# Sums of denominators and the decay of token sums on GpSimd, a half chunk of maxima turned with 128 rows, column sums inverted once

## The chip, the cores and the metric

The kernel runs on one core of a Trainium2 chip. The metric is the time of one execution on the device, in microseconds. A core has engines that each run their own instructions in order and wait for one another by semaphores: PE (TensorE), DVE (VectorE), ACT (ScalarE), POOL (GpSimd) and SP (SyncE, here only DMA issues).

## The reference

An attention whose softmax has one extra term in its denominator, followed by a soft mixture of experts with 32 slots (8 experts with 4 slots each). Sizes: 8 batches, 12 heads, 448 tokens, 64 dimensions a head; 3584 tokens of width 768 for the second part; hidden width 1024.

```python
m = max(scores, axis=-1); e = exp(scores - m)
attn = e / (sum(e) + exp(-m) + 1e-09)          # x = attn @ v, heads side by side
logits = x @ phi                               # 3584 x 32
d = exp(logits - logits.max(0)); d /= d.sum(0) + 1e-09     # over the tokens, for each slot
c = exp(logits - logits.max(1)); c /= c.sum(1) + 1e-09     # over the slots, for each token
slot_out[e] = relu((d.T @ x)[e] @ w1[e]) @ w2[e]
out = c @ slot_out
```

## The kernel before

**The attention** is worked off in 48 pairs of heads, six pairs to a batch, three pairs to a group that is loaded together. The 448 tokens of a head lie in chunks of 128, 128, 128 and 64 rows; the fourth, half chunks of both heads of a pair share one tile of 128 rows. For a pair n there are these stages, each a small function:

- `T(n)` turns q and k on PE into a tile of psA (PSUM, three banks, shared with everything tagged "a"); ACT or DVE copies it out (L255, L257).
- `A(n, i)` or `A1(n, i, hl)`: scores in one orientation on PE (L274, L283, L291), and DVE takes the row maxima straight from psA into the tile `wm` (L277, L285, L292). These run about six pairs ahead.
- `W2(g)` and `W3(g)`, once in three steps: PE turns the group's maxima `wm` (three full chunks at L299, the half chunk at L302), ACT copies them to `mT`, and computes exp(-m) into `ec` (L311, L314).
- `AB(n, i)` and `Bk`: scores in the other orientation less the maxima (L359 and L362, L337 and L340) and ACT's exponential (L364, L343). `AB` sets two score matmuls of `A1` around them.
- `AV(n, i, qs)`: e times v on PE into one bank (psV). A column of ones in v gives the sums of e as column D of each of the seven blocks.
- `N1(n)`: ACT copies that bank to `ubuf` (L409; DVE for the last pairs, and none for the very last).
- `N2(n)`: DVE adds 1e-9, the sum and `ec` (L418, one instruction on 128x7) and inverts (L419); POOL multiplies u by the result into x (L423, L427, L428). `on_pool(n)` is true for n < 44; for the last four pairs DVE multiplies.
- `PX(n)`: PE turns x (L449), ACT copies it (L455).
- `V(g)`: POOL copies v of a group into place (L378 to L381).

**The second part**, `P(b)`, goes on beside the attention, one batch behind it, in six steps spread over half steps of the loop: logits (`l_mm`, `l_ev`, `c_max`), their running maximum (`l_turn`, `s_max`), the differences (`c_sub` L507 and `d_sub` L519 on POOL), `exps` and `corr` on ACT, then `both(s_mm, fade, s_add)`: PE computes the batch's token sums (`ps_s`, in psA), `fade` multiplies the accumulator `acc` (128x224) by the decay exp(old maximum - new maximum) (L534, DVE), and `s_add` adds (L557, DVE). `c_turn` turns the second softmax's exponentials, sums them for each token (L551, DVE), adds 1e-9 and inverts (L552, L553) into `crec`, which is read only near the end of the program (L840). The name `eng` in `P` is POOL for the first six batches and DVE for the last two. After the last pair come the experts (`hidden`, `turn`, `slots`) and the output.

**The order of the work is written out by hand.** Every engine's instructions run in the order in which the loop emits them: for s in 0 to 47 and y in 0 and 1, the scores of pair s, AV of pair s-1 or s, at y = 0 `N1(s-1)`, at y = 1 `T(s+6)`, once in three steps (s = 2, 5, 8, ...) `W2` and `W3`, the step of `P` that is due (`post`), and then `N2(s-1)`, since it is on POOL. At the end of a step POOL gets its loads and copies: at s = 2, 5, 8, ... q and k of a group (two DMA issues, L162); at s = 3, 6, 9, ... `V` of a group, v of the next (two issues, L166 and L167) and, for most of them, a half of a weight (L111); at s = 1, 4, 7, ... another half of a weight. These DMA issues are POOL instructions of 0.7 to 0.8 us each. `s_mm`, `fade` and `s_add` of batch b come at y = 1 of s = 6b + 10.

In `wm` the half chunks of the two heads lie in one column, head 1 in rows 0 to 63 and head 0 in rows 64 to 127.

Of the kernel before, what the change touches and what calls it, by code (L numbers as in the profile page):

```python
# [8 lines left out]
F32 = mybir.dt.float32  # L9
BF16 = mybir.dt.bfloat16  # L10
AX = mybir.AxisListType
AF = mybir.ActivationFunctionType
ALU = mybir.AluOpType
# [12 lines left out]
NP = 3  # L26
# [5 lines left out]
def kernel(  # L32
# [10 lines left out]
    nc = tc.nc  # L43
    B, H, S, D = q.shape
    DD = H * D
    NS = moe_phi.shape[1]
# [3 lines left out]
    KC = DD // 128  # L50
# [15 lines left out]
    crec = keep.tile([128, B, 4], F32, name="crec")  # L66
    acc = keep.tile([128, KC + 1, NS], F32, name="acc")

    ident = const.tile([128, 128], BF16, name="ident")
# [5 lines left out]
    halfm = const.tile([128, 2], F32, name="halfm")  # L75
# [67 lines left out]
    with ExitStack() as at:  # L143
        pool = lambda name, bufs, **kw: at.enter_context(tc.tile_pool(name=name, bufs=bufs, **kw))
        psm = pool("small", 2)
# [77 lines left out]
        nc.gpsimd.memset(ones, 1.0)  # L223
        nc.gpsimd.memset(ones[64:128, 1:2], 0.0)

        ec, mT, eT, av, us = {}, {}, {}, {}, {}
        qkT = {}
        st = {"e2": 0}

# [32 lines left out]
        mg = lambda n: 0 if n == 0 else n // NP + 1  # L262
# [32 lines left out]
        def W2(g):  # L295
            w = wm[g % 2]
            ps = pb_("ps_m")
            for i in range(3):
                nc.tensor.matmul(ps[:, i * 128:(i + 1) * 128], w[:, i, :], ident, start=True, stop=True)  # L299
            for hl in range(2):  # L300
                r = slice(64 - 64 * hl, 128 - 64 * hl)
                nc.tensor.matmul(ps[64 * hl:64 * hl + 64, 384:448], w[r, 3, 0:64], ident[r, r], start=True, stop=True)  # L302
            st["ps_m"] = ps

        def W3(g):
            t = psm.tile([128, S], BF16, tag="mT", name="mT")
            nc.scalar.copy(t, st["ps_m"][:, 0:S])
            mT[g] = t
            e = psm.tile([128, NP, 7], F32, tag="ec", name="ec", bufs=3)
            w = wm[g % 2]  # L310
            nc.scalar.activation(e[:, :, 0:6].rearrange("p l (i h) -> p i l h", i=3),  # L311
                                 w[:, 0:3, :].rearrange("p i (h c) -> p i c h", h=2)[:, :, 0:NP, :],
                                 AF.Exp, scale=-scale)
            nc.scalar.activation(e[:, :, 6], w[:, 3, 0:NP], AF.Exp, scale=-scale)  # L314
            ec[g] = e


# [83 lines left out]
        on_pool = lambda n: n < NPAIR - 4  # L401

        def N1(n):
            src = av[n][:, 0:7 * W65].rearrange("p (s c) -> p s c", c=W65)
            if n == NPAIR - 1:
                us[n] = src
                return
            u = ubuf[:, n % 2, :].rearrange("p (s c) -> p s c", c=W65)
            (nc.scalar.copy if on_pool(n) else nc.vector.tensor_copy)(u, src)  # L409
            us[n] = u  # L410

        def N2(n):
            g, pl = divmod(n, NP)
            b, pb = divmod(n, PB)
            u = us[n]
            eng = nc.gpsimd if on_pool(n) else nc.vector
            rec = psm.tile([128, 7], F32, tag="rec", name="rec", bufs=3)
            nc.vector.scalar_tensor_tensor(rec, u[:, :, D], 1e-9, ec[mg(n)][:, pl, :], op0=ALU.add, op1=ALU.add)  # L418
            nc.vector.reciprocal(rec, rec)  # L419
            x = xb[b % 2]  # L420
            c = pb * 128
            rec2 = psm.tile([128, 2], F32, tag="rec2", name="rec2", bufs=3)
            eng.tensor_mul(  # L423
                x[:, 0:3, c:c + 128].rearrange("p i (h d) -> p i h d", h=2),
                u[:, 0:6, 0:D].rearrange("p (i h) d -> p i h d", h=2),
                rec[:, 0:6].rearrange("p (i h) -> p i h", h=2).unsqueeze(3).to_broadcast([128, 3, 2, D]))
            eng.tensor_scalar(rec2, halfm, rec[:, 6:7], None, op0=ALU.mult)  # L427
            eng.tensor_mul(  # L428
                x[:, 3, c:c + 128].rearrange("p (h d) -> p h d", h=2),
                u[:, 6, 0:D].unsqueeze(1).to_broadcast([128, 2, D]),  # L430
                rec2.unsqueeze(2).to_broadcast([128, 2, D]))
# [30 lines left out]
        def P(b):  # L462
            l, new = lb[b % 2], lb[(b + 1) % 2][:, 4, :]
            eng = nc.gpsimd if b < B - 2 else nc.vector
            x = xb[b % 2]
            v = {}
# [64 lines left out]

            def fade():
                if b:
                    nc.vector.tensor_mul(acc, acc, v["corr"].unsqueeze(1).to_broadcast([128, KC + 1, NS]))  # L534

            def s_mm(j0=0, j1=KC + 1):
                ps = pa([128, j1 - j0, NS], F32, "ps_s")
# [8 lines left out]
            def c_turn():  # L546
                ps = pa([128, 128], BF16, "ps_ct")
                nc.tensor.transpose(ps, flat(v["cd"][:, 0:4, :]), ident)
                nc.vector.tensor_copy(cT[:, b // 2, :, b % 2, :], ps.rearrange("p (h j) -> p h j", h=2))
                r = crec[:, b, :]  # L550
                nc.vector.reduce_sum(r, v["cd"][:, 0:4, :], axis=AX.X)  # L551
                nc.vector.tensor_scalar(r, r, 1e-9, None, op0=ALU.add)  # L552
                nc.vector.reciprocal(r, r)  # L553

            def s_add():
                if b:
# [89 lines left out]
        for s in range(NPAIR):  # L646
            for y in range(2):
                hs = 2 * s + y
                early, last_ = int(hs < 5), int(hs < 3)
                if early:  # L650
                    As(1)
                    Bk(s, 2 * y)
                    warm(int(hs < 2), S)
                    As(1)
                    Bk(s, 2 * y + 1)
                    warm(int(hs < 2), S)
                    As(1)
                elif s < NPAIR:
                    AB(s, 2 * y)
                    if y:  # L660
                        Bk(s, 3, 1)
                    else:
                        AB(s, 1)
                if hs < 5:
                    T(hs + 3)
                if y == 0:
                    if 0 <= s - 1:
                        for i in (2, 3):
                            AV(s - 1, i, range(3))
                else:  # L670
                    if 2 <= s < NPAIR - 6:
                        T(s + 6)
                    g = (s + 1) // 3
                    if (s + 1) % 3 == 0 and g < NG:
                        W2(g + 1)
                        W3(g + 1)
                    if s < NPAIR:
                        for i in (0, 1):
                            AV(s, i, range(3))
                if 2 * s + y in post:  # L680
                    post[2 * s + y]()
                if hs == 2 * (NPAIR - 2) + 1:
                    nc.vector.reduce_max(fold, ident.rearrange("p (i s) -> p s i", i=4), axis=AX.X)
                if y and 0 <= s - 2 < NPAIR - 2 and s - 2 != n6:
                    PX(s - 2)
                if hs == 2 * n6 + 4:
                    PX(n6)
                if y == 0:
                    if 0 <= s - 1:
                        for i in range(4):  # L690
                            AV(s - 1, i, [3])
                        N1(s - 1)
                        if not on_pool(s - 1):
                            N2(s - 1)
                else:
                    if 0 <= s - 1 and on_pool(s - 1):
                        N2(s - 1)
                As(last_)
                if hs == 1:
                    W2(1)  # L700
                    W3(1)
            g = (s + 10) // 3
            if s == 1 or s % 3 == 2:
                g = 3 if s == 1 else g
                if (s == 1 or g > 3) and g < NG:
                    load(g, "q")
                    load(g, "k")
            g = (s + 9) // 3
            if s % 3 == 0 and g - 2 < NG:
                V(g - 2)  # L710
                if s and g - 1 < NG:
                    load(g - 1, "v")
            if s == 1:
                load(2, "v")
            if s == 0:
                for z in range(2, 4):
                    narrow(z)
            if s in half_at:
                load_half(half_at[s], 0, w_tile(half_at[s]))
            if s - 2 in half_at:  # L720
                load_half(half_at[s - 2], 1)
            if s in narrow_at:
                narrow(narrow_at[s])
            for i, z0, z1 in part_at.get(s, ()):
                load_part(i, z0, z1)
            for i, z0, z1 in col_at.get(s, ()):
                load_first(i, z0, z1)
        n = NPAIR - 1
# [3 lines left out]
        AV(n, 3, range(4))  # L732
        load_second(0, 4)
        N1(n)
        N2(n)
        PX(n - 1)
        last[0]()
# [47 lines left out]
        h = [h0, h1]  # L785
# [50 lines left out]
        for half in range(2):  # L836
            ps = psA.tile([128, 512], F32, tag="a", name="ps_cs")
            r = slice(64 * half, 64 * half + 64)
# [57 lines left out]
```

## Time and profile before

| | |
|---|---|
| runs | 308.66, 308.94, 310.42 us (median 308.94) |
| profiled execution | 309.52 us, its span 307.7 us |
| mean granted TensorE clock | 0.955 |
| busy of the span | PE 91%, DVE 84%, ACT 82%, POOL 60% |
| L418 and L419 on DVE | 48 x 0.154 and 48 x 0.201 us |
| L423, L427, L428 on POOL | 44 x 0.823, 0.286 and 0.398 us |
| L534 on DVE | 7 x 0.382 us |
| L552 and L553 on DVE | 8 x 0.170 and 8 x 0.178 us |
| L302 on PE | 34 x 0.213 us |

The span runs from the first to the last instruction; the rest of the execution's time lies around it. A line of the order of time gives start, time from the start of the first to the end of the last of a run of like instructions, engine, line, operation, output and input with their shapes, and in square brackets how long the engine sat idle before it and what ended that. The chain that ended last is followed back from the last instruction, at each step to what released it. The 30 to 225 us in which the loop has its full set of work is called the steady part here.

### The profile page before, as it was taken

The numbers are of one execution on the slowest core, as the hardware profiler recorded it, in microseconds if no ns is written. First come the engines' busy times: TensorE is split into PE (matmuls) and PEld (weight loads), VectorE is DVE, ScalarE is ACT, GpSimd is POOL, SyncE is SP. The second block draws the span as 40 slices with busy tenths as digits, with TensorE's granted clock in tenths as the row PEclk, the third lists the DMA queues.
The fourth block names the chain that finished last, engine by engine and source line by source line (L and its number), as shares of the span: only waits on it lengthen the run. The fifth ranks groups of instructions, "written<-read, shape, count | busy, mean of one in ns | idle before, by whom it ended". The sixth has DMA issues, their size and how long they took to land.

```text
span 307.7 us, 12173 instructions
## 1 busy us (share of the span) xinstructions
PE 279.3 (91%) x5097; PEld 159.8 (52%) x5097; DVE 257.1 (84%) x604; ACT 250.9 (82%) x551; POOL 184.9 (60%) x336
## 2 busy tenths in 40 slices
PE   7999999999999999999999999999999999995900
PEld 2444656566565656555656565656564555441100
DVE  7899999999999999989999999999999676446910
ACT  3477999999999999989999999999999995345800
POOL 9681986968586869866877677686747662000000
PEclk9999999999999999999999999999999999997555
DMA  8999999999999999999999999999845899909995
GB/s 134 134 158 184 139 210 202 195 197 165 191 161 198 164 200 148 202 184 151 120 202 134 197 179 204 151 200 205 141 56 88 124 137 224 362 32 341 433 426 229
DMA packets 49384, 57.69 MB, mean 188 GB/s; under 512 B 2865, under 2 KB 41521, under 8 KB 48945
## 3 DMA queue, kind: packets, MB, share of 16 engines
q0 software_dynamic: 45280, 42.29, 89.6%
q1 hardware_dynamic: 4048, 14.62, 12.1%
q8 instruction: 40, 0.66, 0.8%
q14 instruction: 16, 0.12, 0.1%
HBM read 88.18 MB, written 14.16 MB: 333 GB/s over the span
## 4 chain that ended last, share of the span: by engine, by line
PE 69%; DVE 14%; ACT 8%; issue 3%; POOL 1%; DVEq 0%; POOLq 0%
PE ps_av L397 15%; PE ps_a L291 9%; PE ps_t L251 7%; PE ps_b L359 7%; PE ps_b L362 6%; DVE R L292 6%; PE ps_b L337 4%; PE ps_b L340 2%; ACT R L343 2%; DVE R L277 2%; PE ps_x L449 2%; PE ps_o L802 2%; PE ps_a L274 2%; PE ps_so L773 2%; ACT R L255 2%
## 5 line engine op out<-in xcount | busy, mean ns | idle before, releaser
L292 DVE TENSOR_REDUCE R<-ps_a 128x1 bf16<-128x448 f32 x254 | 140.0, 615 | 6.4 <-PE ps_a L291 5.5
L364 ACT ACTIVATE R<-ps_b 128x448 bf16<-128x448 f32 x272 | 131.0, 573 | 0.5 <-PE ps_b L362 0.2
L291 PE MATMUL ps_a<-R 64*128 64x448 bf16 x254 | 83.2, 353 | 1.5 <-DVE R L292 1.5
L359 PE MATMUL ps_b<-R 64*128 64x448 bf16 x272 | 74.5, 353 | 1.1
L362 PE MATMUL ps_b<-mT,sel 64*128 64x448 bf16 x272 | 71.3, 350 | 0.0
L423 POOL TENSOR_TENSOR R<-ubuf,rec 128x384 bf16<-128x384 f32 x44 | 36.2, 823 | 55.1 <-DVE rec L419 33.7
L397 PEld LDWEIGHTS <-R 128*128 128x128 bf16 (+1 forms) x1536 | 50.0, 100 | 30.8 <-issue 26.1
L397 PE MATMUL ps_av<-R 128*128 128x65 bf16 (+1 forms) x1536 | 64.6, 196 | 0.0
L343 ACT ACTIVATE R<-ps_b 128x448 bf16<-128x448 f32 x64 | 35.9, 579 | 2.7 <-PE ps_b L340 2.6
L251 PEld LDWEIGHTS <-R 64*64 64x64 bf16 x1344 | 30.0, 112 | 12.6 <-issue 4.9
L455 ACT CAST R<-ps_x 128x512 bf16<-128x512 f32 x47 | 28.1, 599 | 6.9 <-PE ps_x L449 6.4
L251 PE MATMUL ps_t<-ident,R 64*64 64x64 bf16 x1344 | 31.2, 196 | 0.6
L285 DVE TENSOR_REDUCE R<-ps_a 128x1 bf16<-128x448 f32 x48 | 29.6, 617 | 0.6 <-PE ps_a L283 0.6
L362 PEld LDWEIGHTS <-sel 64*128 64x128 bf16 x272 | 21.8, 94 | 15.1 <-issue 5.5
L291 PEld LDWEIGHTS <-R 64*128 64x128 bf16 x254 | 23.8, 94 | 11.1 <-issue 1.1
L409 ACT COPY ubuf<-ps_av 128x455 f32<-128x455 f32 x44 | 25.1, 570 | 2.4 <-POOL R L428 2.2
L255 ACT COPY R<-ps_t 128x896 bf16<-128x896 bf16 x20 | 18.4, 922 | 6.0 <-PE ps_t L251 5.6
L337 PE MATMUL ps_b<-R 64*64 64x448 bf16 (+1 forms) x112 | 21.9, 375 | 0.0
L277 DVE TENSOR_REDUCE R<-ps_a 128x1 bf16<-128x448 f32 x34 | 18.9, 618 | 2.1 <-PE ps_a L274 2.0
L340 PE MATMUL ps_b<-mT,sel 64*64 64x448 bf16 (+1 forms) x112 | 20.5, 353 | 0.0
L428 POOL TENSOR_TENSOR R<-ubuf,rec 128x128 bf16<-128x128 f32 x44 | 17.5, 398 | 3.7
L359 PEld LDWEIGHTS <-R 64*128 64x128 bf16 x272 | 17.2, 94 | 4.7 <-issue 0.3
(137 smaller groups left out, 439.7 us busy)
## 6 DMA issues: line engine op xcount, KB each, us to landing
W<-in_moe_w_dram POOLq DMA_DIRECT2D x22, 768.0 KB, 10.2
R<-in_v_dram POOLq DMA_DIRECT2D x32, 192.0 KB, 4.9
out_dram<-W SPq DMA_DIRECT2D x2, 2688.0 KB, 11.8
R<-in_q_dram POOLq DMA_DIRECT2D x14, 336.0 KB, 7.9
R<-in_k_dram POOLq DMA_DIRECT2D x14, 336.0 KB, 9.0
wd<-in_moe_w_dram POOLq DMA_DIRECT2D x8, 384.0 KB, 10.7
R<-wd SPq DMA_DIRECT2D x8, 384.0 KB, 8.2
R<-in_moe_w_dram POOLq DMA_DIRECT2D x2, 768.0 KB, 8.1
```

The costliest lines, as they stand in the source:

```text
L251: nc.tensor.transpose(ps[r, a, c:c + 64], src[r, pl, tok * D:(tok + 1) * D], ident[r, r])
L285: nc.vector.reduce_max(top(n, i), ps[:, 0:S], axis=AX.X)
L291: nc.tensor.matmul(ps[:, 0:S], t[r, 0, i * 128:(i + 1) * 128], t[r, 1, :], start=True, stop=True)
L292: nc.vector.reduce_max(top(n, i, hl), ps[:, 0:S], axis=AX.X)
L337: nc.tensor.matmul(outs[hl], t[rs[hl], 1, cols], t[rs[hl], 0, :], start=True, stop=False)
L343: nc.scalar.activation(e, p[:, 0:S], AF.Exp, scale=scale)
L359: nc.tensor.matmul(ps[hl][:, 0:S], t[rs[hl], 1, cols], t[rs[hl], 0, :], start=True, stop=False)
L362: nc.tensor.matmul(ps[hl][:, 0:S], sel[rs[hl], pl:pl + 1].to_broadcast([64, 128]), mT[mg(n)][rs[hl], :], start=False, stop=True)
L364: nc.scalar.activation(e[:, hl, :], ps[hl][:, 0:S], AF.Exp, scale=scale)
L397: nc.tensor.matmul(o, eT[n, i, hl][:, qc], vp[g % 2][:, 2 * pl + hl, i, 0:W65], start=(i == 0 and u == 0 and hl == 0), stop=(i == 3), skip ...
L423: eng.tensor_mul(x[:, 0:3, c:c + 128].rearrange("p i (h d) -> p i h d", h=2), u[:, 0:6, 0:D].rearrange("p (i h) d -> p i h d", h=2), rec[: ...
L455: nc.scalar.copy(xT[:, pb, :], pss[0])
```

## The change

- In `W2`, the half chunk is turned by two matmuls over all 128 rows of `wm`, each picking its 64 rows by 64 columns of the identity, instead of two over 64 rows.
- `W3` ends with POOL adding 1e-9 to `ec`.
- A new `N2a(n)` adds the sums to `ec`, on POOL for n < 44 and on DVE for the last four. It is emitted right after `N1`, half a step ahead of `N2`. `N2` begins with DVE's inversion and is otherwise as before.
- `fade` runs on `eng`, so on POOL for batches 1 to 5 and on DVE for batches 6 and 7 (batch 0 has none).
- `c_turn` only sums; the last one adds 1e-9 and inverts for all eight batches at once (128x32).

```diff
@@ W2
             for hl in range(2):
-                r = slice(64 - 64 * hl, 128 - 64 * hl)
-                nc.tensor.matmul(ps[64 * hl:64 * hl + 64, 384:448], w[r, 3, 0:64], ident[r, r], start=True, stop=True)
+                c = 64 - 64 * hl
+                nc.tensor.matmul(ps[64 * hl:64 * hl + 64, 384:448], w[:, 3, 0:64], ident[:, c:c + 64], start=True, stop=True)
@@ W3
             nc.scalar.activation(e[:, :, 6], w[:, 3, 0:NP], AF.Exp, scale=-scale)
+            nc.gpsimd.tensor_scalar(e, e, 1e-9, None, op0=ALU.add)
             ec[g] = e
@@ N2
+        def N2a(n):
+            rec[n] = psm.tile([128, 7], F32, tag="rec", name="rec", bufs=3)
+            (nc.gpsimd if on_pool(n) else nc.vector).tensor_add(rec[n], us[n][:, :, D], ec[mg(n)][:, n % NP, :])
+
         def N2(n):
...
-            rec = psm.tile([128, 7], F32, tag="rec", name="rec", bufs=3)
-            nc.vector.scalar_tensor_tensor(rec, u[:, :, D], 1e-9, ec[mg(n)][:, pl, :], op0=ALU.add, op1=ALU.add)
-            nc.vector.reciprocal(rec, rec)
+            r = rec[n]
+            nc.vector.reciprocal(r, r)
@@ fade
-                    nc.vector.tensor_mul(acc, acc, v["corr"].unsqueeze(1).to_broadcast([128, KC + 1, NS]))
+                    eng.tensor_mul(acc, acc, v["corr"].unsqueeze(1).to_broadcast([128, KC + 1, NS]))
@@ c_turn
-                r = crec[:, b, :]
-                nc.vector.reduce_sum(r, v["cd"][:, 0:4, :], axis=AX.X)
-                nc.vector.tensor_scalar(r, r, 1e-9, None, op0=ALU.add)
-                nc.vector.reciprocal(r, r)
+                nc.vector.reduce_sum(crec[:, b, :], v["cd"][:, 0:4, :], axis=AX.X)
+                if b == B - 1:
+                    nc.vector.tensor_scalar(crec, crec, 1e-9, None, op0=ALU.add)
+                    nc.vector.reciprocal(crec, crec)
@@ the loop, y == 0 (and the same line after the last pair)
                         N1(s - 1)
+                        N2a(s - 1)
                         if not on_pool(s - 1):
                             N2(s - 1)
```

## Prediction before the run

> **What bounds the kernel now.** I read first the busy times and the chain that ended last, then the busy times in stretches of 15 us, then POOL, DVE and PE in order of time through one step. The page:
>
> ```profile
> PE 279.3 (91%) x5097; PEld 159.8 (52%) x5097; DVE 257.1 (84%) x604; ACT 250.9 (82%) x551; POOL 184.9 (60%) x336
> PE 69%; DVE 14%; ACT 8%; issue 3%; POOL 1%; DVEq 0%; POOLq 0%
> L423 POOL TENSOR_TENSOR R<-ubuf,rec 128x384 bf16<-128x384 f32 x44 | 36.2, 823 | 55.1 <-DVE rec L419 33.7 <-ACT R L364 9.1 <-ACT R L255 7.1
> ```
>
> PE carries the chain, with 14% handed to DVE. POOL looks as if it had room: 60% busy, and 55.1 us of waiting before its multiplications, mostly for DVE's reciprocal. The stretches show how tight the others are (PE, PEld, DVE, ACT, POOL busy, then granted clock, DMA share, GB/s):
>
> ```profile
> 150.00:165.00 15.00, 14.88 (x319) 9.71 (x319) 14.06 (x34) 14.04 (x33) 10.63 (x21) 1.00 1.10 177
> ```
>
> From 30 to 225 us, PE, DVE and ACT are each busy 13 to 15 us of every 15. Six pairs take 30.25 us (reciprocal of pair 24 at 149.19, of pair 30 at 179.44), so a step is 5.04 us on average. The average hides what decides here, namely that POOL's work comes in bursts. In POOL's order of time, from the multiplications of pair 23 to those of pair 24:
>
> ```profile
> 144.44 0.82 POOL L423 TENSOR_TENSOR R<-ubuf,rec 128x384 bf16<-128x384 f32 x1 [0.79 <-DVE rec L419]
> 145.25 0.28 POOL L427 TENSOR_SCALAR rec<-halfm,rec 128x2 f32<-128x2 f32 x1
> 145.62 0.40 POOL L428 TENSOR_TENSOR R<-ubuf,rec 128x128 bf16<-128x128 f32 x1
> 145.96 0.66 POOL L378 COPY R<-R 128x576 bf16<-128x576 bf16 x1
> 146.68 0.66 POOL L379 COPY R<-R 128x576 bf16<-128x576 bf16 x1
> 147.29 0.34 POOL L380 COPY R<-R 64x192 bf16<-64x192 bf16 x1
> 147.69 0.34 POOL L381 COPY R<-R 64x192 bf16<-64x192 bf16 x1
> 147.98 0.73 POOL L166 DMA_DIRECT2D R<-in_v_dram  x1
> 148.70 0.67 POOL L167 DMA_DIRECT2D R<-in_v_dram  x1
> 149.35 0.78 POOL L111 DMA_DIRECT2D W<-in_moe_w_dram  x1
> 150.20 0.82 POOL L423 TENSOR_TENSOR R<-ubuf,rec 128x384 bf16<-128x384 f32 x1
> ```
>
> The last line waited for nothing but its own queue: pair 24's reciprocal was done at 149.39, and POOL was still issuing a weight load until 150.13. In each third step, at the end of steps s = 3, 6, 9 and so on, POOL runs V and the loads for 4.2 us and is late. Today that is free, since what is late is only the scaling of x, which PE reads over 2 us later (pair 24: scaled by 151.78, read from 153.96). DVE and PE at the same time:
>
> ```profile
> 149.00 0.16 DVE L418 SCALAR_TENSOR_TENSOR rec<-ubuf,ec 128x7 f32<-128x7 f32 x1
> 149.19 0.20 DVE L419 RECIPROCAL rec<-rec 128x7 f32<-128x7 f32 x1
> 149.31 2.17 DVE L292 TENSOR_REDUCE R<-ps_a 128x1 bf16<-128x448 f32 x4
> ```
> ```profile
> 149.57 0.54 PE L362 MATMUL ps_b<-mT,sel 64*128 64x448 bf16 x2
> 149.94 0.35 PE L291 MATMUL ps_a<-R 64*128 64x448 bf16 x1
> ```
>
> PE's fourth score matmul after the reciprocal starts at 149.94, 0.18 after its place in the 0.19 us rhythm (149.57 + 0.19 = 149.76) and right after the first reduction (about 149.31 to 149.85): it needs that bank of psA. So behind the reciprocal there is no slack; whatever delays it delays PE.
>
> **The sum of the denominators (N2a), the main part.** It takes 44 L418 instructions of 0.155 us from DVE and puts 44 adds on POOL, issued right after the ACT copy, and one add of 128x21 for each group. DVE's reciprocal then waits for POOL, and behind it in DVE's order stand the next six reductions of L292, which free psA for PE. In POOL's order the add stands behind all that the last step put there, so in the third steps behind the burst. An add of 128x7 on POOL is not in the trace. The nearest rows are 0.286 us (128x2 TENSOR_SCALAR) and 0.398 (128x128 TENSOR_TENSOR); the two TENSOR_TENSOR sizes (0.398 and 0.823 for 384) extrapolate to 0.19 for none. I take 0.30, with ends 0.19 and 0.40. To it come 0.07 from POOL's last instruction (150.13 to 150.20) and about 0.10 to reach DVE (the other way it is 0.15: 144.28 to 144.44). So the new reciprocal starts 0.47 after POOL is free:
>
> | pair | POOL free | reciprocal now | then | late |
> |---|---|---|---|---|
> | 3 | 44.87 | 43.99 | 45.34 | 1.35 |
> | 6 | 58.90 | 58.03 | 59.37 | 1.34 |
> | 9 | 73.82 | 73.45 | 74.29 | 0.84 |
> | 12 | 88.89 | 88.02 | 89.36 | 1.34 |
> | 18 | 120.00 | 118.26 | 120.47 | 2.21 |
> | 24 | 150.13 | 149.19 | 150.60 | 1.41 |
> | 30 | 180.39 | 179.44 | 180.86 | 1.42 |
> | 36 | 210.63 | 209.68 | 211.10 | 1.42 |
>
> Together 11.3 us. The delay does not depend on where the step begins: POOL's burst itself starts from the previous reciprocal (0.20 + 0.15 + 1.52 of multiplications + 4.2 + 0.47 = 6.5 us from reciprocal to reciprocal, against 5.1 now). In the two other steps of three POOL is free in time, or nearly; pairs 1, 11, 20 and 35 come 0.7 to 0.9 late, of which 0.34 is free (at 144.28, after pair 23's reciprocal, DVE itself waits 0.34 for PE). I count 1.6 for these.
>
> **The decay (fade) on POOL.** Five of the seven L534 (0.38 us) leave DVE, those of batches 1 to 5. Each stands in POOL's order directly behind N2a of pairs 15, 21, 27, 33, 39, again third steps, and DVE's s_add (L557) waits for it, ahead of the reciprocal.
>
> ```profile
> 163.96 0.38 DVE L534 TENSOR_TENSOR acc<-acc,corr 128x224 f32<-128x224 f32 x1
> 164.44 0.39 DVE L557 TENSOR_TENSOR acc<-acc,ps_s 128x224 f32<-128x224 f32 x1
> 164.75 0.16 DVE L418 SCALAR_TENSOR_TENSOR rec<-ubuf,ec 128x7 f32<-128x7 f32 x1
> ```
>
> On POOL, 128x224 lies between the rows of 0.398 and 0.823. From L428 to L423 the time grows by 1.66 ns an element (0.56 for 224), from L507 (128 elements, 0.415) to L519 (160, 0.539) by 3.9 (0.79); I take 0.65. The reciprocal then starts 0.07 + 0.30 + 0.65 + 0.10 + 0.31 (s_add, 164.44 to 164.75) = 1.43 after POOL is free: pair 15, 104.04, late 1.71; pair 21, 133.56, late 0.30 (no weight load there); pair 27, 166.29, late 2.78; pair 33, 195.45, late 1.70; pair 39, 224.94, late 0.95. Together 7.4 us. The Trainium skill (GPSIMD Engine Reference, section Engine selection) calls two-input elementwise work about 2x slower on GpSimd than on VectorE. The rows here say 1.36 to 1.47 (398 to 293, 823 to 558 ns). By the page's factor the fade would be an estimated 0.76, and five of them 0.5 us more in all.
>
> **What is won.** The chain passes through DVE right where the column sums are inverted:
>
> ```profile
> 139.63 0.17 DVE L552 TENSOR_SCALAR crec<-crec 128x4 f32<-128x4 f32 x1
> 139.83 0.18 DVE L553 RECIPROCAL crec<-crec 128x4 f32<-128x4 f32 x1
> ```
>
> These 0.35 and the L418 behind them (0.15) go in six steps (pairs 10, 16, ... 40); PE waited only 0.24 for DVE there before its own work is next late, so I take 0.35 each, 2.1 us. L418 alone in the six steps of pairs 7, 13, ... 37, where the chain also runs through DVE: 0.15 each, 0.9. Elsewhere L418 was off the chain (ACT and PE). The one inversion at the end (128x32, about 0.4 for both instructions) stands under the hidden layer's matmuls: nothing; without that cover 0.1.
>
> **The half chunk (L302).** Two matmuls of 64 rows become two of 128 rows; the chain gives them 0.15 us beside 0.27 for the three before. Ends: 0 and 0.15 for 15 groups in the steady part; I take 0.10, 1.5 us. The Trainium skill (TensorEngine Tiling (Array Packing), Key Properties) says that changing the tiling mode drains the array. Its rule would put the gain near the upper end, 2.3 us; that moves the sum by 0.8.
>
> **Sum.** Lost 11.3 + 1.6 + 7.4 = 20.3; I take nine tenths of it for PE (some steps have a little slack, and a gap of 1.02 us in POOL's burst of pair 27 may close): 18.3. Won 2.1 + 0.9 + 1.5 = 4.5. Net +13.8 on the profiled execution's 309.5 (span 307.7): 323.3. The median of the runs is 308.9, 0.6 lower; I give **323**. With POOL's unknowns at their ends (13 adds by -0.11 or +0.10, five fades by -0.25 or +0.17) and between seven and ten tenths reaching PE, 316 to 328.
>
> **Rivals.**
> - *Half absorbed.* The steps after a late one catch up, because DVE has about 0.5 us less to do in them and PE finds three full banks emptied back to back. For it: DVE's work falls by 11 us in all. Against: after pair 24 the chain is PE's own work (150.11 to 154.12), which starts late. Half of 20.3 less 4.5 gives +5.7: 315 (311 to 317).
> - *Faster.* POOL's add is in time, or its lateness is covered by psA: three banks hold 3 x 0.54 = 1.6 us of reductions. This decides where PE has over 1.4 us of other work ready, before it needs a fourth bank. Then only the 4.5 won is left: 304.5 (302 to 307). For it: two steps in three, where POOL waited for DVE. Against: 149.94 above, where PE already waits for that bank.
> - *No difference.* About a quarter of the delay reaches PE, equal to what is won: 309.
>
> **Chances.** Forecast 0.66, half absorbed 0.15, no difference 0.07, faster 0.12. A measurement tells 0.5% (1.5 us) from no change. Faster 0.12, same 0.07, slower 0.81. The range takes in the forecast's spread and most of the half-absorbed case: 310 to 330, leaving out the faster case, part of no difference, and a longer tail if several steps lose more than POOL's lateness.
>
> **What would show it.** The reciprocal of pairs 3, 6, 9 ... starts right after a POOL add, with DVE idle 1 to 3 us before it, released by POOL: some 15 to 20 us in the table of waits. In the five fade steps DVE waits at s_add instead. POOL's 33.7 us of waiting for the reciprocal shrinks in those steps. Cycles from reciprocal to reciprocal: 6.5 in the third steps, 7.5 or more with a fade. DVE's busy time falls by about 11 us. The forecast is wrong if the add lands before the burst, if an add takes far from 0.3, or if DVE waits and PE's span does not grow with it.

## The result, and the profile after

The changed kernel takes 325.8 us (median; 322.9 to 329.2) against 309.0 before: a ratio of 1.050, 95% interval 1.042 to 1.059. Ratios here and below are of mean times, and executions over 1.5% above the fastest of their kernel (here 329.2 us) are left out of them, so they differ a little from the quotient of the medians. The profiled execution took 326.76 us, its span 325.0, so 17.3 us more of span than before. Line numbers below are those of the kernel that is named; in the changed kernel the add is L415, the reciprocal L423, the multiplications L427, L431 and L432, the decay L538 and s_add L561. The page after:

```profile
PE 283.7 (87%) x5096; PEld 160.8 (49%) x5097; DVE 250.0 (77%) x541; ACT 251.9 (78%) x551; POOL 201.8 (62%) x402
PE 48%; POOL 22%; DVE 15%; ACT 5%; issue 4%; DMA 1%; DVEq 0%; POOLq 0%
L427 POOL TENSOR_TENSOR R<-ubuf,rec 128x384 bf16<-128x384 f32 x44 | 36.3, 826 | 15.4 <-DVE rec L423 14.6
```

DVE works 7.1 us less, PE about the same, and yet the span is longer. The chain says where the time went: POOL's share of it rose from 1% to 22%, at 62% busy. The line of the multiplications shows the other side of it: POOL now waits 14.6 us for the reciprocal and not 33.7. The same stretch of 15 us as before (PE, PEld, DVE, ACT, POOL busy, then clock, DMA share, GB/s):

```profile
150.00:165.00 15.00, 14.13 (x292) 8.92 (x291) 12.86 (x28) 13.56 (x31) 11.18 (x24) 1.00 0.99 145
```

All three of PE, DVE and ACT now stand still for part of it. The waits of DVE name the cause (us in total, times, longest):

```profile
DVE rec L423 <- POOL rec L415: 13.6, 16, 1.8
DVE acc L561 <- POOL acc L538: 8.8, 4, 2.8
```

POOL in order of time, from the multiplications of pair 23 to those of pair 24, the step that the prediction showed:

```profile
153.15 0.83 POOL L427 TENSOR_TENSOR R<-ubuf,rec 128x384 bf16<-128x384 f32 x1 [0.35 <-DVE rec L423]
...
156.70 0.74 POOL L166 DMA_DIRECT2D R<-in_v_dram  x1
157.44 0.67 POOL L167 DMA_DIRECT2D R<-in_v_dram  x1
158.09 0.78 POOL L111 DMA_DIRECT2D W<-in_moe_w_dram  x1
158.94 0.20 POOL L415 TENSOR_TENSOR rec<-ubuf,ec 128x7 f32<-128x7 f32 x1
159.45 0.83 POOL L427 TENSOR_TENSOR R<-ubuf,rec 128x384 bf16<-128x384 f32 x1 [0.31 <-DVE rec L423]
```

The add is the last of the queue, without a wait of its own: ACT's copy, which it needs, ended at 156.47, and the add then stood behind the rest of V and three DMA issues until 158.94. (The points stand for six lines left out: the other multiplications and the copies of V.) DVE and PE in the same time:

```profile
157.53 0.62 DVE L257 COPY R<-ps_t 128x896 bf16<-128x896 bf16 x1
159.17 0.20 DVE L423 RECIPROCAL rec<-rec 128x7 f32<-128x7 f32 x1 [1.02 <-POOL rec L415]
159.29 2.17 DVE L292 TENSOR_REDUCE R<-ps_a 128x1 bf16<-128x448 f32 x4
```
```profile
158.64 0.54 PE L363 MATMUL ps_b<-mT,sel 64*128 64x448 bf16 x2
159.92 0.35 PE L291 MATMUL ps_a<-R 64*128 64x448 bf16 x1 [0.75 <-DVE R L292]
```

One late instruction of 0.20 us on POOL holds 0.20 us on DVE, which holds the reductions, which hold PE's fourth score matmul: 159.92 against a place of 158.83 in the rhythm. From reciprocal to reciprocal this step took 6.29 us, against 5.11.

**A cost that the prediction did not have** is in the clock. Behind two of the longer standstills of PE (1.53 us ahead of 126.28, 2.10 ahead of 177.28) the matmuls of 448 columns take 0.56 to 0.58 us each and not 0.35, for 3.4 us. In slices of one microsecond, some of those after the first of the two (the granted clock is the seventh number from the left, behind POOL's count):

```profile
127.00:128.00 1.00, 1.00 (x36) 0.91 (x32) 0.82 (x2) 0.24 (x1) 1.00 (x2) 0.63 0.90 113
128.00:129.00 1.00, 1.00 (x10) 0.29 (x6) 0.69 (x2) 0.57 (x2) 0.26 (x2) 0.50 1.08 186
130.00:131.00 1.00, 1.00 (x33) 0.94 (x29) 0.61 (x3) 0.57 (x2) 0.00 (x0) 0.67 1.08 195
```

The clock is granted at half from 127.25 to 130.67, and the cycle that it falls into is 1.3 us longer (pair 19: 6.62; pair 28: 6.18; with the clock at full the same cycles take 5.32 and 4.84, as a run below shows).

**Where the 17.3 us are**, from the cycles between reciprocals of the two profiles: third steps without a decay (pairs 3, 6, 9, 12, 18, 24, 30, 36) +9.5; with a decay (15, 21, 27, 33, 39) +5.8; other steps in which the add is late, less those slightly shorter, +3.8; two stretches of half clock +2.6; the steps of pairs 4, 7, 10, 13 and so on, where less is left on DVE and a little is caught up, -4.7; start and end +0.2.

### The profile page after: what moved, and what is told of

Read it like the earlier page. It is cut to its first block, busy times and chain, and to the rows that moved or that the text cites. A ratio compares the mean times of both kernels' runs of the same rounds, so it can differ in the third digit from the quotient of the medians.

```text
span 325.0 us, 12162 instructions
## 1 busy us (share of the span) xinstructions
PE 283.7 (87%) x5096; PEld 160.8 (49%) x5097; DVE 250.0 (77%) x541; ACT 251.9 (78%) x551; POOL 201.8 (62%) x402
## 4 chain that ended last, share of the span: by engine, by line
PE 48%; POOL 22%; DVE 15%; ACT 5%; issue 4%; DMA 1%; DVEq 0%; POOLq 0%
PE ps_av L398 10%; DVE R L292 8%; PE ps_a L291 7%; PE ps_t L251 5%; PE ps_b L360 4%; PE ps_b L363 3%; POOL R L166 3%; PE ps_b L338 3%; POOL R L380 3%; POOL W L111 3%; POOL R L167 2%; PE ps_o L808 2%; POOL R L427 2%; PE ps_a L274 2%; POOL R L379 2%
## 5 line engine op out<-in xcount | busy, mean ns | idle before, releaser
L292 DVE TENSOR_REDUCE R<-ps_a 128x1 bf16<-128x448 f32 x254 | 140.6, 617 | 8.4 <-PE ps_a L291 6.2
L365 ACT ACTIVATE R<-ps_b 128x448 bf16<-128x448 f32 x272 | 132.7, 584 | 6.1 <-PE ps_b L363 5.8
L291 PE MATMUL ps_a<-R 64*128 64x448 bf16 x254 | 84.9, 356 | 14.4 <-DVE R L292 8.3
L360 PE MATMUL ps_b<-R 64*128 64x448 bf16 x272 | 75.3, 356 | 1.0
L427 POOL TENSOR_TENSOR R<-ubuf,rec 128x384 bf16<-128x384 f32 x44 | 36.3, 826 | 15.4 <-DVE rec L423 14.6
L344 ACT ACTIVATE R<-ps_b 128x448 bf16<-128x448 f32 x64 | 36.7, 592 | 3.5 <-PE ps_b L341 3.5
L251 PEld LDWEIGHTS <-R 64*64 64x64 bf16 x1344 | 30.8, 113 | 14.2 <-issue 7.4
L251 PE MATMUL ps_t<-ident,R 64*64 64x64 bf16 x1344 | 32.1, 198 | 1.3 <-issue 0.6
L291 PEld LDWEIGHTS <-R 64*128 64x128 bf16 x254 | 23.9, 94 | 11.2 <-issue 1.1
L315 POOL TENSOR_SCALAR ec<-ec 128x21 f32<-128x21 f32 x17 | 4.7, 275 | 36.3 <-ACT ec L314 36.3
L360 PEld LDWEIGHTS <-R 64*128 64x128 bf16 x272 | 16.8, 94 | 12.0 <-issue 7.6
```

Source lines behind the costliest of these rows:

```text
L251: nc.tensor.transpose(ps[r, a, c:c + 64], src[r, pl, tok * D:(tok + 1) * D], ident[r, r])
L291: nc.tensor.matmul(ps[:, 0:S], t[r, 0, i * 128:(i + 1) * 128], t[r, 1, :], start=True, stop=True)
L292: nc.vector.reduce_max(top(n, i, hl), ps[:, 0:S], axis=AX.X)
L344: nc.scalar.activation(e, p[:, 0:S], AF.Exp, scale=scale)
L360: nc.tensor.matmul(ps[hl][:, 0:S], t[rs[hl], 1, cols], t[rs[hl], 0, :], start=True, stop=False)
L365: nc.scalar.activation(e[:, hl, :], ps[hl][:, 0:S], AF.Exp, scale=scale)
```

## The experiments

The theory was the prediction's: the add and the decay stand in POOL's order behind its bursts, DVE waits for them, and PE for DVE. The rivals: a general price of work moved to POOL (its load, the crossing between engines, contention with DVE), and PE's low clock as a cause of its own.

**The parts alone.** Three kernels, each the kernel before with one part of the change, or with the two that put nothing on POOL.

```diff
@@ e1_sums_only: N2a and the add to ec as changed; fade, c_turn and W2 as before
@@ e2_fade_only
-                    nc.vector.tensor_mul(acc, acc, v["corr"]...
+                    eng.tensor_mul(acc, acc, v["corr"]...
@@ e3_crec_and_turn: c_turn and W2 as changed; N2 and fade as before
```

> Only the sums of the denominators (N2a and the add to ec) on GpSimd; decay, column sums and half chunk as before. Theory (POOL's add stands behind the burst of each third step, DVE's reciprocal waits for it, PE waits for DVE): with the add's measured 0.20 and 0.13 around it, the reciprocal comes 0.33 after POOL is free: eight third steps late by 10.2 us in all, four of the five steps with a decay by 2.9 more, other steps some 2, less 1 to 1.5 for L418: 309 + 13, so 322 (318 to 325), cycles of 6.3 us in the third steps, DVE idle 1.0 before their reciprocals. Rival (the parts only cost together, by load on POOL as a whole): under 314. Rival (it is the decay that costs, not the sums): 309 or less.

Measured 322.4 (ratio 1.040, 1.034 to 1.045; before 309.3). As expected, to 0.4 us. One of its four executions took 1219 us, with every matmul about four times as long (1440 ns for L291); it is not in the ratio, and the cycles are read from a further execution of the same kernel:

> The sums on GpSimd alone, one profile: cycles from reciprocal to reciprocal of 6.3 us in the third steps without exception (with the decay on DVE, those steps too), 5.35 in pairs 13, 19, 25, 31 and 37, the old 5.4 less 0.15 in pairs 10, 16, 22, 28, 34 and 40. Rival (load): all cycles longer by a few per cent.

322.2 us, and cycles that are not longer in general. "Without exception" did not hold: the third steps take 6.27 to 6.29, but for pairs 18 (7.07, with a narrow part in the burst), 27 (7.09), 21 (5.53), 39 (5.78) and 42 (6.00), where the burst is longer or shorter; 5.32 to 5.33 in pairs 13, 25, 31 and 37, 5.23 to 5.25 in 10, 16, 22, 28 and 34, 5.74 in 40. Pair 19's 6.68 lies behind a gap of 1.61 us and has the half clock. The load theory falls.

> Only the decay on GpSimd. Theory: s_add waits for POOL in the steps of pairs 15, 27, 33 and 39 by 1.5, 2.6, 1.5 and 0.8 us, pair 21 hardly; less what DVE no longer does: 309 + 5.5, so 314.5 (312 to 317), and one more us if a wait of over 2 us lowers PE's clock. Rival (load on POOL as a whole, which is 3 us here): within 1 us of before. Rival (decay is most of the loss): over 320.

Measured 318.6 (1.027, 1.021 to 1.033), 1.6 us above the expected range, which had allowed one more for the clock. The waits were as expected; in the profile DVE waits for POOL's decay in pair 27's step:

```profile
169.55 0.39 DVE L557 TENSOR_TENSOR acc<-acc,ps_s 128x224 f32<-128x224 f32 x1 [2.71 <-POOL acc L534]
```

The five cycles with a decay are longer by 1.51, 0.13, 2.31, 1.52 and 0.76 us, 6.2 in all; every other cycle up to pair 43 is the old one to 0.01, but pair 28's: 2.35 us longer, behind a standstill of 1.99 us and at half clock, here for 6.8 us. So the wait counted twice, once by itself and once by the clock. Another 1.2 us of that profile come from before the first pair: the clock is at full from 16.8 us there and from 13.9 in the kernel before, and among the profiles of kernels that begin alike the first reciprocal starts between 28.7 and 30.3. Together the two parts cost less than their sum (13.1 and 9.3), since in the third steps with a decay both stand behind the same burst: pair 33's cycle is 0.51 longer with the sums, 1.52 with the decay, 1.45 with both.

> Only the column sums inverted once and the half chunk turned with 128 rows; nothing new on GpSimd. Theory: 0.25 to 0.4 us in each of six steps where the chain runs through the inversions, and up to 0.1 in each of 15 turns: 306.5 (305 to 308). Rival (both are hidden): 309 within 0.7. Rival (128-row tiles cost PE a change of mode): slower than before.

Measured 307.3 (0.992, 0.988 to 0.995): faster than before, in the expected range. The cycles tell which part does it: those of pairs 10, 16, 22, 28, 34 and 40 are 0.39 shorter each, 2.3 in all, and the others with a W2 (pairs 7, 19, 25, 31, 37) are the same to 0.01. Pairs 13 and 21 came 0.19 later, behind standstills of PE that wait for nothing that the profile shows (0.18 us in pair 13's cycle, 0.81 in place of 0.62 in pair 21's). DVE in the step of pair 22, where the prediction showed L552 and L553 ahead of the addition:

```profile
138.85 0.28 DVE L550 TENSOR_REDUCE crec<-cd 128x4 f32<-128x128 bf16 x1
139.04 0.16 DVE L418 SCALAR_TENSOR_TENSOR rec<-ubuf,ec 128x7 f32<-128x7 f32 x1
139.23 0.20 DVE L419 RECIPROCAL rec<-rec 128x7 f32<-128x7 f32 x1
```

So the column sums win 2.3 us, and the half chunk, which no run has alone, wins nothing that shows.

**More and less in front of the add.** V makes one of its copies twice, in the changed kernel and in the one before, and the changed kernel runs once more beside them.

```diff
@@ V, e6_after_plus_copy and e7_before_plus_copy
             nc.gpsimd.tensor_copy(t[:, 1:HG:2, 0:3, 0:D], s[:, 1:HG:2, 0:3, :])
+            nc.gpsimd.tensor_copy(t[:, 1:HG:2, 0:3, 0:D], s[:, 1:HG:2, 0:3, :])
```

> The changed kernel once more, beside the next three. 323 to 326 with a spread of some 3 us. Theory: in the profile PE stands still for 1.4 to 2.1 us in the steps with a decay and in pair 18's, and after some of these gaps its clock is at half for 3.3 us; which of them trip it differs from run to run, so the same pairs' cycles should again come out the same to 0.05 us except behind such gaps.

> All of the change, and V makes one of its copies twice (0.66 us more on POOL in each third step). Theory: the add comes 0.66 later in 13 steps and nothing hides it: 8.6 us more than the changed kernel, 332 to 335, and a little more by low clock. Rival (POOL has room, the loss is a fixed price of the new waits): within 2 us of the changed kernel.

> The kernel before, with the same doubled copy. Theory: nothing that PE waits for stands behind POOL's burst there, so 309 to 310. Rival (POOL's time counts in the kernel before as well, by contention or late x): 2 us or more above before.

The changed kernel: 325.7 (1.052, 1.045 to 1.059). With the copy, 342.5 (1.106, 1.096 to 1.116); the kernel before with the copy, 308.8 beside 308.9 (1.000, 0.997 to 1.003). The same 0.7 us of POOL work in each third step costs nothing where only the scaling of x is late by it, and 16.9 us where the add is. In pair 24's step:

```profile
166.64 0.20 POOL L416 TENSOR_TENSOR rec<-ubuf,ec 128x7 f32<-128x7 f32 x1
```
```profile
166.87 0.20 DVE L424 RECIPROCAL rec<-rec 128x7 f32<-128x7 f32 x1 [1.76 <-POOL rec L416]
```

DVE's wait is 1.76 and not 1.02. Every third step is longer by the copy's 0.73 us (6.30 became 7.03, pair 15's 7.22 became 7.96, pair 27's 8.03 became 8.76), 10.2 in 14 of them. That was to be 332 to 335. The profile is 15.2 us above that of the changed kernel, and the other 5 us are half clock: the cycles of pairs 13, 19, 22, 28, 34 and 43 are 1.2 to 2.1 longer than without it, behind standstills of 1.47 to 2.83 us, against two such cycles in the changed kernel. The expectation had the mechanism right and the size wrong; it named the low clock and gave it too little.

**PE kept busy.** Up to 16 matmuls whose result nobody reads, ahead of two score matmuls. They were meant for those at which PE stands still, but the edit puts them one step of the loop earlier, ahead of the reciprocal that comes late and not behind it.

```diff
@@ AB, e5_pe_kept_busy (fill: y == 0, i == 1, s % 3 == 1 and s < 42)
+            if fill: idle()        # 8 matmuls of 192 columns into a bank of psB
             if run:
                 A1(*run, 0)
...
+            if fill: idle()
             if run:
                 A1(*run, 1)
```

> All of the change, and PE gets up to 16 short matmuls (192 columns, into a bank that nobody reads) ahead of the two score matmuls at which it waits in the third steps. Theory: they fill the standing time, which the wait for POOL makes anyway; no gap is over 1.3 us, the half clock does not come, and the 2.6 us that the profile of the changed kernel lost behind two gaps do not occur: 322 to 324, and the waits of DVE for POOL stay as they are. Rival (the low clock has another cause): low clock in the same places, time as the changed kernel or up to 8 us above it, since the fillers take 0.5 us or so in 13 steps. Rival (PE's own time counts in these steps): 328 or more.

Measured 326.4 (1.056, 1.050 to 1.061), so no gain on the whole. The clock did what was expected of it: the two stretches that had half clock are at full clock, here the one behind pair 18 (it lay at a mean of 0.72 from 126 to 132 in the changed kernel):

```profile
126.00:132.00 6.00, 6.00 (x136) 3.97 (x130) 5.57 (x12) 5.23 (x13) 3.50 (x8) 1.00 1.07 153
```

Pair 19's cycle is 5.32 and pair 28's 4.84, 2.6 us less together. But the fillers did not fill the wait. In pair 24's cycle the second eight of them stand here, the first eight at 154.37, and DVE's reciprocal behind both:

```profile
155.81 0.83 PE L351 MATMUL ps_fill<-phi_sb,ident 128*128 128x192 bf16 x8
```
```profile
160.11 0.19 DVE L432 RECIPROCAL rec<-rec 128x7 f32<-128x7 f32 x1
```

They hold up PE, and with it the six reductions ahead of the reciprocal, until POOL's add (done at 159.60) is in time. DVE's waits for POOL at the add and the decay fell from 22.4 to 6.1 us, where they were expected to stay, and those of L292 for PE rose from 6.2 to 23.2. In pairs 3, 6, 24 and 30 the third step took 6.73 to 6.75 (6.30 without fillers), in pairs 9 and 39 0.7 and 1.05 more. So one wait was exchanged for another. No standstill of PE in the loop is over 0.73 us, and there is no half clock, which speaks for the standstills as its cause; whether fillers in the right place would be free was not tried.

**The adds in time.** In the first of three versions of the whole change, the loads of the third steps come behind the scaling of x; in the second, the loads of the other steps stand behind the add of the next step; in the third, this begins only at step 4.

```diff
@@ e4_loads_after_scaling (s % 3 == 0: V stays, the loads go to a list)
-                    load(g - 1, "v")
+                    later.append(lambda g=g: load(g - 1, "v"))
@@ y == 1, behind N2
                         N2(s - 1)
+                    while later: later.pop(0)()
@@ e8_loads_split: as well, y == 0, for the loads of the steps with s % 3 != 0
                         N2a(s - 1)
+                        while early_: early_.pop(0)()
```

> All of the change, but in the third steps the loads that follow V (v, the half of a weight, one narrow part) are issued in the next step, after POOL's scaling of x, so that the add of the sums and the decay stand behind V only. Theory: POOL is then free 2.2 us earlier, at about the time at which ACT's copy is done; the waits of 1 to 2.8 us go, what is left is the gain: 305 (303 to 308), faster than both. Rival (POOL's adds cost by themselves, as engine time, in crossing between engines or in contention with DVE): at least half of the loss stays, over 316. Rival (late loads then hold up V): DVE's waits move to V's wait for DMA, 310 to 318.

Measured 308.0 (0.995, 0.992 to 0.998): 17.8 us less than the changed kernel's 325.8 for the same instructions in another order, and faster than before, though not the 305 expected. POOL between V and the add of pair 24:

```profile
147.61 0.34 POOL L382 COPY R<-R 64x192 bf16<-64x192 bf16 x1
148.04 0.20 POOL L415 TENSOR_TENSOR rec<-ubuf,ec 128x7 f32<-128x7 f32 x1
149.54 0.82 POOL L427 TENSOR_TENSOR R<-ubuf,rec 128x384 bf16<-128x384 f32 x1 [1.30 <-DVE rec L423]
```

The add is done a microsecond before DVE wants it (149.27), and no gap of PE in the loop is over 0.73 us. So the price was in the order: adds, decay and crossings between engines are all still there. What stays is mostly in other steps, where q and k or parts of weights are loaded ahead of the add: pairs 4, 8, 11, 20, 28, 35 and 42 still wait 0.35 to 1.25.

> The version with the loads of the third steps behind the scaling of x, and now the loads of the other steps too stand behind POOL's add of the next step (q and k, first halves of weights, narrow parts). Theory: the adds that still came late there (pairs 4, 8, 11, 14, 20, 28, 32, 35, by 0.2 to 1.25 us) are in time: 4.3 us less than that version, 304 (302.5 to 305.5), faster than the kernel before by 1.5% and than the one with the column sums alone. Rival (late loads or late scaling of x then hold up the next stage): 307 or more, with new waits in V or in the turning of x.

Measured 310.5 (1.004, 1.002 to 1.006): the rival came true, in one step. Pair 3's cycle was 8.55 and not 5.17:

```profile
36.68 0.41 PE L251 MATMUL ps_t<-ident,R 64*64 64x64 bf16 x14 [0.75 <-DMA R<-in_q_dram]
38.31 0.41 PE L251 MATMUL ps_t<-ident,R 64*64 64x64 bf16 x14 [1.23 <-DMA R<-in_k_dram]
```

Near the start q and k have no time to spare, and PE's standstills for them brought half clock from 39.7 to 43.1 as well. The adds came in time in nearly all other steps.

> The version with the loads split around the adds, but the loads of steps 1 and 2 where they were. Theory: the 3.4 us that pair 3 lost there was PE waiting for q and k, issued one step later at a time when DMA is full; without it the other cycles come out as there: 307.0 (306 to 308), faster than the kernel before by 0.7% and no better than the column sums alone (307.3), since the adds on GpSimd take nothing off the chain but 0.06 to 0.19 in a few steps. Rival (the added waits between engines still cost in the steady part): 309 or more.

Measured 308.3 (0.997, 0.994 to 0.999). Pair 3's cycle is back at 5.23; the time is at the upper end of what was expected or just above. So with the add in time the whole change is worth 1 us, where the column sums with the half chunk gave 2. What the earlier reciprocals win (pairs 10, 16, ... by 0.16 to 0.58) is partly given back in pairs 12, 36 and 42 (0.33 to 0.56 longer), where POOL is still late, and in pair 24 (5.80 for 5.11), where PE's turning of q and k began 0.7 us later for a reason that the profile doesn't show.

> The column sums inverted once and the half chunk of 128 rows, and the addition L418 left out of the computation: the reciprocal takes the sums of e alone, without exp(-m) and 1e-9. This bounds what any place for the addition can win. Theory: DVE is in the chain with it only in the steps of pairs 7, 13, ... and 10, 16, ..., 0.1 to 0.2 each: 306 (305 to 307), 1 us less than with the addition on DVE (307.3). Rival (DVE's busy time is what bounds the steady part): 44 times 0.155, so 300 to 302.

Measured 304.7 (0.985, 0.981 to 0.989), 2.6 us below the version with the addition on DVE, somewhat more than expected. The profile: pairs 16, 22, 28, 34 and 40 are shorter by 0.53 to 0.54 (0.39 with the addition), pairs 17, 23, 29 and 35 by 0.06 to 0.08, the third steps hardly (PE-bound, DVE waits 0.54 for it); pairs 21 and 42 came 0.7 and 0.3 earlier than before. This leaves out the term exp(-m), so it is no version, but a bound: the 48 additions take 7.4 us of DVE (0.154 each), and their complete absence is worth 2.6 by the medians. In the profile 0.7 of the gain is pair 21's cycle, and that is another matter: PE's standstill of 0.62 us in it, which waits for nothing that the profile shows, did not occur in this execution. Without it about 2 are left.

Of all versions that compute everything, the one with the column sums and the half chunk alone (307.3) has the lowest time, though its interval overlaps those of the first and third version here (308.0 and 308.3).

## Why the prediction was right

It gave 323, within 310 to 330, and the mechanism as it happened; the time is 325.8. By its own steps:

- **The sums of the denominators.** Third steps: 11.3 us predicted, 9.5 measured, pair by pair 0.21 to 0.23 less. Two sizes were off in the same direction: the add takes 0.20 there (0.215 on average), not 0.30, and DVE starts 0.03 behind it, not 0.10; POOL also began its burst 0.07 behind the reciprocal before it, not 0.15. The lower end of the bounds, 0.19 from the slope of L428 to L423, was the right one; the two nearest rows (0.286 and 0.398) were far off.
- **"Behind the reciprocal there is no slack."** Right: in pair 24's step DVE stood still for 1.02 us, the add of 0.16 on DVE was gone, and the cycle grew by 1.18. The discount to nine tenths was not needed; the terms that it was applied to came to 19.1 and not 20.3, so the 18.3 came near by chance.
- **Other steps.** 1.6 predicted for pairs 1, 11, 20 and 35; 2.6 measured there, and 1.2 more, net, in pairs 8, 14, 26, 32, 42 and the rest, mostly where POOL's q and k issues end just when the add would be due. Mis-sized, because POOL's freedom in these steps was taken as given when it was only just enough.
- **The decay.** 7.4 predicted, 5.8 measured. L538 takes 0.648 us, the value taken (0.65). The Trainium skill's factor (GPSIMD Engine Reference, section Engine selection) would have given an estimated 0.76: against the 0.382 of DVE's L534 before the measured ratio is 1.7. Pairs 15, 21, 33 and 39 are 0.25 to 0.30 below the prediction, which is the add and the handovers again, and pair 27 is 0.53 below; the prediction had said that a gap in POOL's burst there may close, which would fit.
- **What is won.** 4.5 predicted, 4.7 measured, and this agreement is chance. Pairs 10, 16, ... 40 won 3.4 (2.1 predicted): 2.3 by the column sums, as in the run that has them without the additions, and the rest by the addition. Pairs 7, 13, ... 37 won 1.1 (0.9 predicted), most of it by catching up (below), and pair 4 another 0.2. The half chunk won 0 (1.5 predicted), and that is the term that failed: the turning of W2 takes 0.42 us from its first matmul to AV's in both profiles (pair 22's step, at full clock: 138.12 to 138.54 before, 147.59 to 148.01 after). The rule of the Trainium skill (TensorEngine Tiling (Array Packing), Key Properties) that a change of tiling mode drains the array had been taken as pointing to the upper end; here it made no difference, and the new form is itself a tile of another shape (128*64).
- **Missing altogether:** the half clock behind PE's standstills, 2.6 us in the profile. Without it the profiled execution would have come to 324.1, 0.8 above the 323.3 that the prediction gave for it, where smaller waits in the third steps and larger ones in the others stood against each other. So this cost, for which the prediction had no term, is most of what the forecast was low by.
- **The signs.** DVE's waits for POOL came to 22.4 us (15 to 20 expected), the cycles to 6.3 without a decay, but for pairs 18 (7.08) and 42 (6.02), and to 6.45 to 8.03 with one (6.5, and 7.5 or more, expected). DVE's busy time fell by 7.1 us and not by 11: the 11 added up durations, and neighbouring DVE records overlap by about 0.1 us, so that taking one out frees less.
- **The rivals.** "Half absorbed" failed as the prediction argued: the later steps caught up little. Pairs 4, 7, 13, 25, 31 and 37, behind late steps, are 0.17 to 0.20 shorter than before, and 0.05 to 0.08 in the kernel without the addition, where nothing is late: some 0.1 each. "Faster" named the point from which it decides, other work of over 1.4 us for PE ahead of a fourth bank; PE had about 0.7 us of it in the step shown (from the end of DVE's copy at 158.15 to 158.83) and stood still for the rest.

## What to carry to other kernels

An engine with room on average may still be the worst place for a small instruction that another engine waits for in order: look at what stands ahead of it in that engine's queue at that moment, and measure the burst, not the share. When work is moved, its order on the new engine is part of the change: the same instructions took 325.8 or 308.0 us. And a nearly saturated engine is worth relieving only where the chain runs through it: of 7.4 us taken off DVE, some 2 to 2.6 were to be had at best.

## What the runs showed of the hardware

- In the loop PE's clock is granted at half for 3.4 us, twice for 6.8, behind a standstill shorter than that, and the length of the gap alone does not decide it. It came behind gaps of 1.53 and 2.10 us in the changed kernel, 1.61 with the sums alone, 1.99 with the decay alone and 1.47 to 2.83 with the extra copy; in the repeat of the changed kernel (the profile is of its longest execution, 330.5 us) also behind 1.28 (ahead of 93.80) and 1.43 (ahead of 229.67), and the cycles of pairs 13 and 37 took 6.75 and 6.68 there, not 5.32 and 5.33. It did not come behind other gaps of 1.40 to 1.57 in these kernels, nor behind two of 2.17 and 2.19 with the extra copy (ahead of 114.26 and 239.99).
- Where the gap lies counts too. In each trace all changes of the granted clock stand on one grid of 3.413 us (in the changed kernel it is full from 130.67 to 178.45, which is 14 steps). Between 30 and 272 us of the 13 kept profiles of these kernels and the kernel before that ran at normal speed, each of the 8 grid steps at full clock in which PE stood still for 1.6 us or more in all was followed by half clock, 7 of 16 with 1.28 to 1.57, and none with less. The gaps of 2.17 and 2.19 us were divided by the grid: the steps hold 0.85 and 1.32 us, and 1.44 and 0.75. The Trainium skill (TensorE: Matmul & The Clock Gate, Part 1: The HAM clock gate) describes a free-running window of about 3.4 us and calls one idle window the condition. The length of the slow stretch and the grid agree; but here less than half of a step stood idle in some of the cases, so a whole idle window was not needed.
- One of some 80 executions of these kernels, of the one with the sums alone, ran with all matmuls about four times as long from end to end (1219 us). No run here shows why.
